# Two inverse transforms on TensorE: one 128-column stationary operand per half of 64 rows, in place of two 64x64 quarters

## The chip, the cores and the metric

The kernel runs on one core of a Trainium2 chip. The metric is the device time of one execution in microseconds (us), the median over several runs. The core has a matrix engine (TensorE, PE in the profile, with its loads of the stationary operand kept apart as PEld), a vector engine (VectorE, DVE), a scalar engine (ScalarE, ACT), GpSimd (POOL) and SyncE (SP), whose queue here issues most DMAs.

## What is computed

A filter in the frequency domain, followed by a gated convolution, for 8 sequences of 3200 positions with 256 channels:

```python
X = np.fft.rfft(x, axis=1)
Yr = Xr @ w_r - Xi @ w_i + b_r
Yi = Xr @ w_i + Xi @ w_r + b_i
Yr = np.sign(Yr) * np.maximum(np.abs(Yr) - 0.01, 0.0)      # and the same for Yi
y = np.fft.irfft(Yr + 1j * Yi, n=3200, axis=1)

for k in range(5):                                          # causal, over positions
    gate_pre += conv_w[k] * yp[:, k:k + S, :]
gate = 1.0 / (1.0 + np.exp(-gate_pre))
out = (gate * (y @ w_val)) @ w_out
```

Inputs and outputs are float32.

## The kernel before

The transform of 3200 points is split into 64 x 50. Per batch (`b`, 8 of them) the work goes through five stages; every stage is a list of *pieces*, and the names in brackets are the tiles that the profile shows.

- `p1` (L529, in the first batch `p1_first`, L486): 50-point transforms of the input, 8 pieces (u) per batch. TensorE writes `p` (L543) with 64x64 quarters: a stationary operand of 50 rows and 64 columns, four of which take up the array, and 512 moving columns. ACT copies `p`, and the result goes to DRAM (`a_dram`).
- `p2` (L564), 13 pieces per batch: `a` comes back from DRAM turned round; 64-point transforms (`s`, L590); the mix with `w_r` and `w_i` (`k_ps` L665, `y_ps` L660), bias and shrinkage on DVE and ACT. These matmuls take the whole array, 128 rows by 128 columns.
- `s1i` (L692, inside `p2`): the first transform back, one group for two pieces, 6 per batch. It writes `z_ps` (L703), in two banks. The stationary operand comes from `g1_sb` (two transforms i, in rows 0 to 63 and 64 to 127), the moving one is `tp` with 256 columns. Each product is split in quarters: half of the rows i, half of the columns e. Two products (r = 0 and 1, real and imaginary) are added up. ACT copies `z_ps` to `z_t` (L714), and a DMA stores it to `z_dram`.
- `positions` (L735), 8 blocks (k) per batch: `zl` comes from `z_dram`; `s2i` (L750) is the second transform back into `y_p` (L759). Here the data are the stationary operand: 50 rows in either half h of the array (`half(h)` is the 50 rows from row 64h), 128 channels of one c and one m split in two quarters e, and the 50x50 matrix `g2_sb` moves. ACT copies `y_p` to `y_sb` (L766).
- `gated` (L827): `v_ps` and `o_ps` (L791; in the last blocks L787) on TensorE, five taps of the convolution on ACT and DVE (L810, L813), the gate (L855), and the store.

Both halves of `z_ps` and of `y_p` write different PSUM banks: `p[:, i, ...]` in `s1i`, `pv[h]` in `s2i`. The tag `ps_2` has two slots of two banks, shared by `p`, `z_ps`, `y_p`, `v_ps` and `o_ps`.

The order on each engine is fixed by the program. `Plan.order` (L111) simulates the pieces with a table of costs and of due times (`O`, L230) and then writes them out; each piece is added with its planned time (1776 ns for `s1i`, 950 ns for `s2i`) and a mode, "q" for the pieces of quarters (`p1`, `s1i`, `s2i`) and "f" for full-size matmuls; the planner charges for a switch from one mode to the other (`SWITCH`, L212) and puts "q" pieces next to each other where it can. The change leaves these planned times and modes alone.

Of the kernel before, what the change touches and what calls it, by code (L numbers as in the profile page):

```python
# [17 lines left out]
B, S, D = 8, 3200, 256  # L18
P = 128
HP = P // 2  # L20
# [59 lines left out]
class Plan:  # L80
# [11 lines left out]
    def add(self, at, engine, busy, fn, uses=(), sets=(), new=None, delay=None, mode="r", kb=0, chain=None, extra=0):  # L92
        n = len(self.pieces)
        before = set()
        for key in uses:
            before |= set(self.writers.get(key, ()))
        for key in sets:
            before |= set(self.readers.get(key, ())) | set(self.writers.get(key, ()))
        for key in uses:
            self.readers.setdefault(key, []).append(n)  # L100
        for key in sets:
            self.writers[key], self.readers[key] = [n], []
        p = dict(n=n, at=at, engine=engine, busy=busy, fn=fn, before=before, new=new or {}, mode=mode, kb=kb, extra=extra,
                 tiles={key[:2] for key in (*uses, *sets)}, delay=busy + LAND[engine] if delay is None else delay)
        p["behind"] = {self.last[chain]} if chain in self.last else set()
        if chain:
            self.last[chain] = n
        self.pieces.append(p)
        return n
# [113 lines left out]
def act(n, kind="copy"):  # L223
    return {"copy": 45, "cast": 95, "mul": 104, "conv": 187, "relu": 198, "sigmoid": 103}[kind] + n / 1.2
# [38 lines left out]
def fourier_filter_then_gated_conv(ctx: ExitStack, tc: tile.TileContext, x, w_r, w_i, b_r, b_i,  # L263
                                   w_val, conv_w, w_out, f1, f2, g1, g2, eye, out):
    nc = tc.nc
# [7 lines left out]
    tl = {}  # L273
# [9 lines left out]
    g2_sb = const.tile([P, N2], F32, name="g2_sb")  # L283
# [10 lines left out]
    def buffer(key, tag, shape, dtype=F32):  # L294
        pool = ps if tag.startswith("ps_") else dram if tag.endswith("_dram") else sb
        tl[key] = pool.tile(shape, dtype, name=key[0], tag=tag, bufs=SLOTS[tag])
        return tl[key]
# [7 lines left out]
    def two_banks(key):  # L305
        return buffer(key, "ps_2", [P, 2, 512])
# [172 lines left out]
    def half(h):  # L479
        return slice(h * HP, h * HP + N2)  # L480
# [83 lines left out]
    def p2(b, u, at):  # L564
# [123 lines left out]
        kts = [("tp", (b, v)) for v in both]  # L688
# [3 lines left out]
        def s1i():  # L692
            p = two_banks(kz)
            if last:
                nc.tensor.matmul(p[:, 0, 0:D], g1_sb[:, ts[0] * P:(ts[0] + 1) * P], tl[kt][:, 0, :], start=True, stop=True)
                return
            for j, v in enumerate(both):
                g = g1_sb[:, 2 * v * P:(2 * v + 2) * P].rearrange("p (r q) -> p r q", r=2)

                for r in range(2):  # L700
                    for i in range(2):
                        for e in range(2):
                            nc.tensor.matmul(p[e * HP:(e + 1) * HP, i, j * D:(j + 1) * D],  # L703
                                             g[i * HP:(i + 1) * HP, r, e * HP:(e + 1) * HP],
                                             tl[kts[j]][i * HP:(i + 1) * HP, r, :], start=r == 0, stop=r == 1)
        add(at + O["s1i"], "PE", 430 if last else 1776, s1i, [*[k + (0,) for k in kts], *gs], [kz + (0,)], {kz: "ps_2"}, mode="f" if last else "q")

        def keep():
# [26 lines left out]
    def positions(b, k, at):  # L735

        bk = (b, k)
        kz, kp = ("zl", bk), ("y_p", bk)

        def load():  # L740
            zt = buffer(kz, "zl", [P, MB * D]).rearrange("p (m c) -> p m c", m=MB)
            src = tl["z_dram", b].rearrange("(f h) (m c) -> h f m c", h=NH, c=D)
            for h in range(NH):
                nc.sync.dma_start(out=zt[half(h)], in_=src[h, :, k * MB:(k + 1) * MB, :])
        add(at + O["load_z"], "SP", 700, load, [("z_dram", b, u) for u in range(NU)], [kz + (0,)], {kz: "zl"}, kb=400, chain="zl")

        def views():
            return [tl[kp][:, h, 0:TB].rearrange("p (c m n) -> p c m n", c=2, m=MB) for h in range(NH)]

        def s2i():  # L750
            zt = tl[kz].rearrange("p (m c) -> p m c", m=MB)
            two_banks(kp)
            pv = views()

            for c in range(2):
                for m in range(MB):
                    for h in range(NH):
                        for e in range(2):
                            nc.tensor.matmul(pv[h][e * HP:(e + 1) * HP, c, m, :],  # L759
                                             zt[half(h), m, c * P + e * HP:c * P + (e + 1) * HP], g2_sb[half(h), :],  # L760
                                             start=True, stop=True)

        free = [("turn", "read", (b - 1, j)) for j in range(4)] if k == NB - 1 and b else []
        add(at, "PE", 950, s2i, [kz + (0,), ("g2", 0, 0), *free], [kp + (0,)], {kp: "ps_2"}, mode="q", chain="s2i")
        lo = (k * MB + H0) * N2
        add(at + 0.1, "ACT", act(2 * TB), lambda: nc.scalar.copy(  # L766
            out=y_sb[:, :, :, lo:lo + MB * N2], in_=tl[kp][:, :, 0:TB].rearrange("p h (c n) -> p c h n", c=2)),
            [kp + (0,)], [("y", k, 0)])
        if k < NB - 1:
            return  # L770
        w = H0 * N2
        add(at + 0.1, "DVE", 283, lambda: nc.vector.tensor_copy(out=y_sb[:, :, 1, 0:w], in_=y_sb[:, :, 0, lo:lo + w]),
            [("y", k, 0)], [("y", -1, 0)])

        def turned(c):
            old = y_sb[:, c, 1, lo:lo + w].rearrange("p (m n) -> p m n", n=N2)
            new = y_sb[:, c, 0, 0:w].rearrange("p (m n) -> p m n", n=N2)
            nc.vector.tensor_copy(out=new[:, :, 1:], in_=old[:, :, :N2 - 1])
        for c in range(2):
            add(at + 0.1, "DVE", 171, lambda c=c: turned(c), [("y", k, 0)], [("y", -1, 1 + c)])  # L780
# [158 lines left out]
    for b in range(B):  # L939
# [11 lines left out]
        start = (b + 1) * T + O["p3"] + O.get(f"p3_{b}", 0.0)  # L951
# [33 lines left out]
```

## Time and profile before

| | |
|---|---|
| median of 3 runs | 900.42 us (905.22, 896.17, 900.42) |
| span of the profiled execution, first to last instruction | 897.1 us |
| mean granted TensorE clock | 0.986 |
| TensorE busy / VectorE / ScalarE | 865.2 / 763.5 / 603.7 us |
| `z_ps` (L703) records on TensorE | 1536 |
| `y_p` (L759) records on TensorE | 4096 |

The profile is one execution of its own. Its time outside the span isn't listed; its span lies 3.3 us below the median of the runs. In it, every fp32 matmul of the program (the two transforms back, `p`, `s`) appears as two matmuls, each with a load of its stationary operand (LDWEIGHTS); a matmul on operands of type fp32r (L660, L665, L791) appears once. Matmuls overlap each other, so their durations don't add up to time; the length of a piece in the chain of waits does. A row like `50*64 50x64` gives rows and columns of the array that are used, then the operand.

### The profile page before, as it was taken

What the parts mean: (1) busy time and instruction counts of PE and PEld (TensorE: products, weight loads), DVE (VectorE), ACT (ScalarE), POOL (GpSimd) and SP (SyncE); (2) the same over time, 40 slices, a digit from 0 to 9 for tenths busy, and PEclk for the clock granted to TensorE, in tenths of its full rate; (3) what the DMA queues carried; (4) which work ended last, traced back from release to release, by engine and by line L of the source; (5) the groups of instructions that cost most, each with busy time, mean ns of one, the idle gap of its engine ahead of it and who ended that gap; (6) DMA issues with size and microseconds to landing.
All of it is one profiled execution on the core that took longest, in us unless ns stands there. A gap on an engine that the chain in (4) does not pass through costs nothing.

```text
span 897.1 us, 24381 instructions
## 1 busy us (share of the span) xinstructions
PE 865.2 (96%) x10370; PEld 741.1 (83%) x10370; DVE 763.5 (85%) x1139; ACT 603.7 (67%) x924; POOL 4.4 (0%) x11
## 2 busy tenths in 40 slices
PE   7799979999999999999999999999999999999898
PEld 2478758898888988899888988989788899998675
DVE  1267787999899997999789996999969998999896
ACT  1256656877677867777677876877757776875654
POOL 0000000000000000000000000000001000000000
PEclk8889999999999999999999999999999999999999
DMA  6577777635755476555674566645674453513522
GB/s 203 198 233 239 228 227 217 210 130 182 236 180 179 159 229 218 190 183 160 217 235 158 163 204 217 222 131 174 215 223 154 139 172 109 178 62 116 180 75 91
DMA packets 103439, 162.26 MB, mean 181 GB/s; under 512 B 9154, under 2 KB 77636, under 8 KB 103332
## 3 DMA queue, kind: packets, MB, share of 16 engines
q1 hardware_dynamic: 102372, 157.44, 54.8%
q10 hardware_dynamic: 960, 3.28, 1.1%
q8 instruction: 81, 1.33, 0.6%
q14 instruction: 26, 0.21, 0.1%
HBM read 82.04 MB, written 78.64 MB: 179 GB/s over the span
## 4 chain that ended last, share of the span: by engine, by line
PE 83%; DVE 10%; DMA 4%; ACT 2%; issue 1%; ACTq 1%; SPq 0%
PE y_ps L660 14%; PE o_ps L791 13%; PE v_ps L791 12%; PE s L590 10%; PE z_ps L703 9%; PE k_ps L665 8%; PE y_p L759 7%; PE p L543 6%; DVE acc L813 4%; DMA x<-in_x 1%; PE v_ps L787 1%; DVE acc L855 1%; DVE gated L317 1%; DMA f_sb<-in_f 1%; DMA a_dram<-s 1%
## 5 line engine op out<-in xcount | busy, mean ns | idle before, releaser
L813 DVE SCALAR_TENSOR_TENSOR acc<-y_sb,cw_sb,acc 128x800 f32<-128x800 f32 (+1 forms) x264 | 255.9, 1018 | 17.6 <-ACT acc L810 17.2
L660 PE MATMUL y_ps<-w_sb,xs 128*128 128x256 f32 x1152 | 155.4, 284 | 0.6 <-DVE xs L648 0.6
L791 PE MATMUL o_ps<-gated,wo_sb 128*128 128x400 f32 x756 | 155.2, 351 | 0.6 <-DVE acc L855 0.6
L660 PEld LDWEIGHTS y_ps<-w_sb,xs 128*128 128x128 f32 x1152 | 144.5, 189 | 11.3 <-DVE xs L652 3.2
L791 PEld LDWEIGHTS o_ps<-gated,wo_sb 128*128 128x128 f32 x756 | 133.5, 188 | 3.1 <-DVE acc L855 0.8
L791 PE MATMUL v_ps<-y_hl,wv_sb 128*128 128x400 f32 x660 | 131.3, 346 | 0.5 <-ACT o L879 0.5
L590 PE MATMUL s<-f_sb,a 128*128 128x128 f32 x800 | 113.2, 284 | 8.2 <-ACT wo_sb L315 3.4
L791 PEld LDWEIGHTS v_ps<-y_hl,wv_sb 128*128 128x128 f32 x660 | 118.5, 188 | 1.6 <-ACT o L879 0.9
L590 PEld LDWEIGHTS s<-f_sb,a 128*128 128x128 f32 x800 | 101.7, 196 | 20.8 <-issue 6.9
L678 ACT ACTIVATE tp<-yb,nlam 128x512 f32<-128x512 f32 (+1 forms) x104 | 73.7, 708 | 38.7 <-DVE yb L674 38.6
L665 PEld LDWEIGHTS k_ps<-w_sb,xs 128*128 128x128 f32 x576 | 77.2, 190 | 20.8 <-issue 10.5
L703 PE MATMUL z_ps<-tp,g_sb 64*64 64x256 f32 x1536 | 93.4, 381 | 0.0
L665 PE MATMUL k_ps<-w_sb,xs 128*128 128x256 f32 x576 | 91.1, 294 | 1.2 <-DVE yb L671 0.9
L759 PEld LDWEIGHTS y_p<-g_sb,zl 50*64 50x64 f32 x4096 | 68.3, 135 | 18.1 <-issue 7.3
L315 ACT CAST gated<-acc 128x800 fp32r<-128x800 f32 x63 | 54.3, 862 | 38.2 <-DVE acc L855 38.0
L759 PE MATMUL y_p<-g_sb,zl 50*64 50x50 f32 x4096 | 72.5, 219 | 7.1 <-issue 4.2
L680 DVE SCALAR_TENSOR_TENSOR tp<-yb,tp 128x512 f32<-128x512 f32 (+1 forms) x104 | 70.0, 673 | 10.6 <-ACT tp L678 10.5
L671 DVE TENSOR_TENSOR yb<-k_ps,bias_sb 128x512 f32<-128x512 f32 x96 | 65.6, 684 | 15.7 <-PE k_ps L665 15.6
L703 PEld LDWEIGHTS z_ps<-tp,g_sb 64*64 64x64 f32 x1536 | 55.3, 133 | 27.4 <-issue 5.1
L855 DVE TENSOR_TENSOR acc<-v_ps,acc 128x800 f32<-128x800 f32 x64 | 62.9, 984 | 16.1 <-PE v_ps L791 12.7
L674 DVE TENSOR_TENSOR yb<-y_ps,yb 128x512 f32<-128x512 f32 x96 | 65.5, 683 | 7.4 <-PE y_ps L660 6.9
L714 ACT COPY z_t<-z_ps 128x1024 f32<-128x1024 f32 x48 | 48.5, 1010 | 25.7 <-PE z_ps L703 25.1
(80 smaller groups left out, 1016.7 us busy)
## 6 DMA issues: line engine op xcount, KB each, us to landing
zl<-z_dram SPq DMA_DIRECT2D x128, 200.0 KB
out<-o SPq DMA_DIRECT2D x63, 400.0 KB
a<-a_dram SPq DMA_DIRECT2D x96, 256.0 KB
z_dram<-z_t SPq DMA_DIRECT2D x48, 512.0 KB
x<-in_x SPq DMA_DIRECT2D x120, 200.0 KB
a_dram<-s SPq DMA_DIRECT2D x120, 200.0 KB
x<-in_x ACTq DMA_DIRECT2D x8, 200.0 KB
a_dram<-s ACTq DMA_DIRECT2D x8, 200.0 KB
```

Source lines behind the costliest of these rows:

```text
L590: nc.tensor.matmul(spec()[:, c, :, i, :], tl[ka][:, i, c * P:(c + 1) * P], f2_of(i), start=True, stop=True)
L660: nc.tensor.matmul(p[:, 1 - r, :], xm(hx, c, r), w_sb[:, m, hw, c, :], start=k == 0, stop=k == 5)
L665: nc.tensor.matmul(p, sm(hx, c), w_sb[:, 0, hw, c, :], start=k == 0, stop=k == 5)
L671: nc.vector.tensor_tensor(out=buffer(kb, "yb", [P, 2, D]), in0=tl[kk].rearrange("p (a d) -> p a d", a=1).to_broadcast([P, 2, D]), in1=bias ...
L674: add(at + 0.2, "DVE", dve(2 * D), lambda: nc.vector.tensor_tensor(out=yb(), in0=tl[ky], in1=yb(), op=ALU.add), [ky + (0,)], [kb + (0,)])
L678: nc.scalar.activation(out=buffer(kt, "tp", [P, 2, D])[:, 0:n], in_=tl[kb][:, 0:n], func=AF.Relu, bias=nlam)
L680: add(at + 0.2, "DVE", dve(n * D), lambda: nc.vector.scalar_tensor_tensor(out=tl[kt][:, 0:n], in0=tl[kb][:, 0:n], scalar=LAM, in1=tl[kt][: ...
L703: nc.tensor.matmul(p[e * HP:(e + 1) * HP, i, j * D:(j + 1) * D], g[i * HP:(i + 1) * HP, r, e * HP:(e + 1) * HP], tl[kts[j]][i * HP:(i + 1) ...
L759: nc.tensor.matmul(pv[h][e * HP:(e + 1) * HP, c, m, :], zt[half(h), m, c * P + e * HP:c * P + (e + 1) * HP], g2_sb[half(h), :], start=True ...
L791: nc.tensor.matmul(p[:, e, 0:TB], w[:, hw, c, e * P:(e + 1) * P], src(hy, c), start=n == 0, stop=n == 5)
L813: nc.vector.scalar_tensor_tensor(out=acc(c), in0=y_of(c, j), scalar=cw_sb[:, c, j:j + 1], in1=acc(c), op0=ALU.mult, op1=ALU.add)
L855: add(at + O["gate"], "DVE", dve(2 * TB), lambda: nc.vector.tensor_tensor(out=gate(), in0=hn(tl[kv][:, :, 0:TB]), in1=gate(), op=ALU.mult) ...
```

## The change

Where `s1i` and `s2i` issued two matmuls for the two halves e of the stationary operand's columns, they issue one with all 128 columns, in the same half of rows. The output of each goes to all 128 partitions of PSUM. The sums, their order and the data are the same.

```diff
@@ s1i
                 for r in range(2):
                     for i in range(2):
-                        for e in range(2):
-                            nc.tensor.matmul(p[e * HP:(e + 1) * HP, i, j * D:(j + 1) * D],
-                                             g[i * HP:(i + 1) * HP, r, e * HP:(e + 1) * HP],
-                                             tl[kts[j]][i * HP:(i + 1) * HP, r, :], start=r == 0, stop=r == 1)
+                        nc.tensor.matmul(p[:, i, j * D:(j + 1) * D], g[i * HP:(i + 1) * HP, r, :],
+                                         tl[kts[j]][i * HP:(i + 1) * HP, r, :], start=r == 0, stop=r == 1)
@@ s2i
             for c in range(2):
                 for m in range(MB):
                     for h in range(NH):
-                        for e in range(2):
-                            nc.tensor.matmul(pv[h][e * HP:(e + 1) * HP, c, m, :],
-                                             zt[half(h), m, c * P + e * HP:c * P + (e + 1) * HP], g2_sb[half(h), :],
-                                             start=True, stop=True)
+                        nc.tensor.matmul(pv[h][:, c, m, :], zt[half(h), m, c * P:(c + 1) * P], g2_sb[half(h), :], start=True, stop=True)
```

Nothing moves against anything else on any engine; the groups at the two lines have half as many matmuls with twice the columns. The rows of TensorE's program, in the first batch where `z_ps` stands between two groups of `p` (a row gives line, tile and operands, output shape and the number of the program's matmuls in a row). Before:

```order
L424 MATMUL turned<-eye_sb,f_sb 128x128 x2
L543 MATMUL p_796<-x,f_sb 64x512 x4
L703 MATMUL z_ps<-tp,g_sb 64x256 x16
L543 MATMUL p_832<-x,f_sb 64x512 x4
L665 MATMUL k_ps<-w_sb,xs 128x256 x6
```

and with the change:

```order
L424 MATMUL turned<-eye_sb,f_sb 128x128 x2
L543 MATMUL p_772<-x,f_sb 64x512 x4
L702 MATMUL z_ps<-tp,g_sb 128x256 x8
L543 MATMUL p_800<-x,f_sb 64x512 x4
L665 MATMUL k_ps<-w_sb,xs 128x256 x6
```

The places are the same; `z_ps` has outputs of 128 partitions now, while its neighbours `p` keep 64. Later, in a batch with `y_p` groups, next to each other and next to `p`. Before:

```order
L660 MATMUL y_ps<-w_sb,xs 128x256 x12
L759 MATMUL y_p<-g_sb,zl 64x50 x64
L665 MATMUL k_ps<-w_sb,xs 128x256 x6
L759 MATMUL y_p<-g_sb,zl 64x50 x32
L543 MATMUL p_5702<-x,f_sb 64x512 x4
L590 MATMUL s_5712<-f_sb,a 128x2x64 x4
```

and with the change:

```order
L660 MATMUL y_ps<-w_sb,xs 128x256 x12
L756 MATMUL y_p<-g_sb,zl 128x50 x32
L665 MATMUL k_ps<-w_sb,xs 128x256 x6
L756 MATMUL y_p<-g_sb,zl 128x50 x16
L543 MATMUL p_5062<-x,f_sb 64x512 x4
L590 MATMUL s_5072<-f_sb,a 128x2x64 x4
```

A group of `y_p` has 16 matmuls in place of 32, at the same place. Over the whole program there are 64 groups of `y_p` and 48 of `z_ps` of this form, 33 of the latter right behind full-size matmuls; a group of `p` comes right behind one of them 24 times, and one of them right behind `p` 12 times.

## Prediction, made before the changed kernel ran

> **What bounds the kernel now.** I read the page's first part, the busy time by stretch, and then the chain of waits for the stretch in which the two transforms back run. First the page:
>
> ```profile
> span 897.1 us, 24381 instructions
> PE 865.2 (96%) x10370; PEld 741.1 (83%) x10370; DVE 763.5 (85%) x1139; ACT 603.7 (67%) x924; POOL 4.4 (0%) x11
> ```
>
> TensorE leads, but VectorE at 85% could be the limit somewhere. The view by stretch separates the two; its columns are the stretch, its length, then each engine's busy time with the number of its instructions, the granted clock and the DMA share:
>
> ```profile
> 60.00:100.00 40.00, 40.00 (x408) 33.63 (x407) 25.12 (x46) 26.83 (x48) 0.00 (x0) 1.00 0.75 237
> ...
> 300.00:400.00 100.00, 100.00 (x1281) 88.98 (x1280) 91.12 (x134) 74.59 (x114) 0.00 (x0) 1.00 0.61 194
> ...
> 700.00:800.00 100.00, 99.51 (x1433) 93.53 (x1431) 94.23 (x139) 71.34 (x113) 0.00 (x0) 1.00 0.44 141
> 800.00:870.00 70.00, 64.90 (x834) 53.72 (x834) 66.34 (x82) 44.61 (x59) 0.00 (x0) 1.00 0.36 118
> ```
>
> A busy TensorE may still be one that is not needed, so the chain of waits decides. Its summary for 135 to 794 us, and for 794 to 868 us:
>
> ```profile
> by line: PE y_ps L660 17.0%; PE v_ps L791 16.6%; PE o_ps L791 16.1%; PE s L590 11.8%; PE z_ps L703 10.9%; PE k_ps L665 9.6%; PE y_p L759 8.2%; PE p L543 6.0%; issue 0.7%; PE y_ps L623 0.7%; PE y_ps L624 0.6%; PE z_ps L695 0.4%; DVE gated L3
> ...
> by line: DVE acc L813 44.0%; DVE acc L855 11.4%; DVE gated L317 8.2%; PE y_p L759 6.0%; issue 4.9%; ACT acc L824 4.3%; DVE y_hl L317 4.1%; DVE tp L680 3.2%; ACT acc L810 2.6%; DVE yb L674 2.5%; DVE yb L671 1.6%; DVE xs L648 1.6%; ACT y_sb L
> ```
>
> In the long middle the chain is TensorE line after line: whatever a group there takes more or less moves the end by as much. In the 74 us of the second row VectorE leads and TensorE waits, apart from the y_p groups (6.0%). Both edited lines, L703 and L759, stand on the first chain.
>
> **The edit itself** replaces two matmuls of 64 stationary columns by one of 128. For each of the two, the question is what a step costs: the moving operand streaming through, or the stationary operand being loaded. From the view of groups by line:
>
> ```profile
> L590 PE MATMUL s<-f_sb,a 128*128 128x128 f32 x800 | 113.2, 284 | 8.2 <-ACT wo_sb L315 3.4
> L590 PEld LDWEIGHTS s<-f_sb,a 128*128 128x128 f32 x800 | 101.7, 196 | 20.8 <-issue 6.9
> L703 PE MATMUL z_ps<-tp,g_sb 64*64 64x256 f32 x1536 | 93.4, 381 | 0.0
> L703 PEld LDWEIGHTS z_ps<-tp,g_sb 64*64 64x64 f32 x1536 | 55.3, 133 | 27.4 <-issue 5.1
> L759 PE MATMUL y_p<-g_sb,zl 50*64 50x50 f32 x4096 | 72.5, 219 | 7.1 <-issue 4.2
> L759 PEld LDWEIGHTS y_p<-g_sb,zl 50*64 50x64 f32 x4096 | 68.3, 135 | 18.1 <-issue 7.3
> ```
>
> The profile counts two matmuls and two loads for each fp32 matmul of the program: 48 groups of 32 at L703, 64 groups of 64 at L759. The means are durations with a fixed delay in them, not costs in a stream. Costs in a stream come from the chain, where consecutive pieces add up without overlap (start, length, what):
>
> ```profile
> 72.31 1.73 PE z_ps L703 x32
> ...
> 401.51 0.89 PE s L590 x8
> ...
> 403.80 1.89 PE z_ps L703 x32
> 405.69 0.92 PE y_p L759 x64
> 406.61 1.09 PE s L590 x8
> ...
> 423.53 1.02 PE p L543 x8
> 424.55 1.61 PE y_ps L660 x12
> ...
> 428.05 0.86 PE p L543 x8
> 428.91 0.90 PE k_ps L665 x6
> ...
> 432.89 1.40 PE y_ps L660 x12
> ...
> 436.48 0.70 PE k_ps L665 x6
> ```
>
> **The z_ps step is streaming.** With four quarters side by side a group has 8 steps: 1.73 / 8 = 0.216 us. The s row streams 128 columns in 0.89 / 8 = 0.111 us at most, so 256 columns need about 0.22. Nothing is left over for loading. With two halves side by side there are again 8 steps of 256 columns. The load of 128 columns, at most the 0.111 of an s step, fits behind 0.216. I take zero for the stream; the bounds are zero and the 0.111 of an uncovered load per step, and that end is a rival below.
>
> **The y_p step is loading.** 64 records are 16 steps of four quarters: 0.92 / 16 = 0.0575 us. Streaming 50 columns at the s rate is 50/128 of 0.111 = 0.043, so it doesn't fill the step. The timeline of the loads alone, in windows that widen, shows what does (start, from the first start to the last end, number):
>
> ```profile
> 403.73 0.15 PEld L703 LDWEIGHTS z_ps<-tp,g_sb 64*64 64x64 f32 x4
> ...
> 403.73 0.21 PEld L703 LDWEIGHTS z_ps<-tp,g_sb 64*64 64x64 f32 x8
> ...
> 406.54 0.19 PEld L590 LDWEIGHTS s<-f_sb,a 128*128 128x128 f32 x1
> ...
> 406.54 0.30 PEld L590 LDWEIGHTS s<-f_sb,a 128*128 128x128 f32 x2
> ```
>
> Four loads of 0.133 end within 0.15, so they start within 0.02 of each other, and the next four end 0.06 later. A load of 128 columns ends 0.11 behind the one before. The durations agree: 196 - 133 = 63 ns more for 64 more columns. So 64 columns cost about 0.055, and four such loads are done in 0.06: they run at the same time, the two quarters of one half of rows included. One load of 128 columns in place of that pair does one after the other what was done at once: about 0.111 in place of 0.0575. The program's group keeps 16 steps (two halves in place of four quarters), so it becomes 16 x 0.111 = 1.78 us, **0.86 more**. Bounds for a step: 0.043, the streaming, below which nothing goes, and 0.222, two loads of halves in series. I take 0.111, because the nearest row, the s load, has the same type and the same 128 columns.
>
> The Trainium skill's page "TensorE: Matmul & The Clock Gate", section "LDWEIGHTS (loading the stationary operand)", gives columns / 1.2 ns whatever the number of rows; an estimate from it is 107 ns for 128 columns and 53 for 64, and the load rows above agree. By it the step would gain 0.05 and the sum be 4 us lower. The page "TensorEngine Tiling (Array Packing)", section "Restrictions", speaks for the change: tiling by columns switches Fast Weight Load off. The first page allows that mode only for types other than FP32, and the s loads, 128 columns without column tiles, show no trace of it; if it held here, the time would be that of the first rival below.
>
> How many groups count? The view of L759 alone by stretch:
>
> ```profile
> 100.00:800.00 700.00, 62.98 (x3584) 59.84 (x3584) 1.00 0.58 185
> 800.00:868.00 68.00, 9.54 (x512) 8.46 (x512) 1.00 0.37 122
> ```
>
> 3584 / 64 = 56 groups lie before 800, on TensorE's chain. Of the 8 behind, these are on the chain:
>
> ```profile
> 834.09 2.08 PE y_p L759 x128
> 836.19 1.19 PE y_p L759 x64
> ...
> 855.39 1.19 PE y_p L759 x64
> ```
>
> Those are four; the other four stand beside VectorE's taps (L813) and are covered. 60 x 0.86 = **51.6 us**. If none of the last eight counted it would be 48.2, with all of them 55.0.
>
> **Switches of shape.** In the chain rows a group of quarters behind full-size matmuls costs 0.16 more (p 1.02 against 0.86, z_ps 1.89 against 1.73), and full-size matmuls behind quarters 0.20 more (k_ps 0.90 against 0.70, s 1.09 against 0.89, y_ps 1.61 against 1.40). Today p, z_ps and y_p have one shape; afterwards p keeps its quarters and the others have halves. By the order of the program on TensorE there are 36 places where p meets one of them, 24 into p and 12 out of it. The trace has no switch between quarters and halves. It is bounded by nothing and by these rows; I take the rows, since the switch today changes both sizes and its cost depends on the width loaded next: 24 x 0.16 + 12 x 0.20 = **6.2 us**. The 33 z_ps groups behind full-size matmuls load 128 columns first, 0.04 more each by the same two rows: **1.3 us**.
>
> **What hides nothing.** ACT's copy of y_p (L766) starts 0.86 later, and behind it in ACT's queue stand the casts and the first tap. In the middle ACT is busy 75 of 100 us and TensorE has other groups in line, so I cost it at nothing; without that cover TensorE would wait out another 0.86 per group, up to 52 us. Half the instructions at the edited lines save no time, since neither step is limited by issue.
>
> **The sum.** 51.6 + 6.2 + 1.3 = 59.1 us on the profiled span of 897.1, so 956.2. The listed runs are 905.22, 896.17 and 900.42 us; the profiled execution lies 3.3 below their median, and I carry that offset: **960 us**.
>
> **Rivals.**
> *The load is no longer the limit (faster).* Should a half's 128 columns load in 0.043 or less, y_p steps become streaming: 16 x (0.043 - 0.0575) = -0.23 a group, -14 over 60, and 887 us if the switches cost nothing. It decides at the 0.0575 that a step takes today. For it speaks only that no load in this shape is in the trace; against it the 0.11 of the s load, which holds in a stream. 0.04.
> *The change doesn't change the step.* If the two quarters of a half already loaded in turn, at 0.028 each, the load of 128 columns takes the same 0.0575. Only 36 switches at 0.16 stay: 906 us. Against it: 0.028 for 64 columns would be half the s load's rate. 0.06.
> *Halves in series.* If loads of the two halves can't run at once, a y_p step is 0.222: 16 x (0.222 - 0.0575) x 60 = +158; z_ps loads just fit. With the switches 1066 us. The trace has no halves; that quarters of different rows load at once speaks against it. 0.04.
> *A load can't begin while its own half streams.* Then y_p steps are 0.111 + 0.043 = 0.154, +93 us, and z_ps steps get 0.111 more, 8 x 0.111 x 48 = +43; 1043 us with the switches. The z_ps steps speak against it: 0.216 is all streaming, with 256 columns and a load in it. 0.04. The page on TensorE, section "What overlaps and what doesn't", states just this rule, that a load overlaps matmuls only of another row group; this trace disagrees with it, by that 0.216.
>
> **How the numbers follow.** The forecast has 0.82. Its own range: without switches and with none of the last eight groups 900.4 + 48.2 + 1.3 = 950; the 0.30 - 0.19 = 0.11 of the loads' timeline, good to its last digit, leaves a step of 0.107 open, 4 us less in all, 946; and the listed runs scatter by 5 either way: 940 at the low end. With all eight groups 963, with scatter 968, and with a fifth of ACT's 52 us uncovered 980. That leaves the rivals' 0.18 out, so it is the whole range. A difference under about 1% can't be told from none here. Faster by over 1%: 0.04; within 1%: 0.06; slower by over 1%: 0.90.
>
> **What will show it.** Behind the change y_p should have 2048 records, loads of about 190 ns, and groups of 32 in about 1.8 us of the chain; z_ps groups 16 records in 1.7 to 1.9 as now; p groups behind z_ps 1.02 in place of 0.86. VectorE's share should fall to about 80%. The forecast is wrong if y_p groups stay near 0.9, or z_ps groups leave 1.9.

## The result, and the profile after

The changed kernel takes 962.25 us (median of 4 runs, 959.2 to 966.26), the kernel before 898.84 us in the same comparison: a ratio of 1.0689, interval 1.0621 to 1.0757. The profiled execution has a span of 958.7 us in a run of 960.48. The page's first part, and its groups at the two edited lines (`y_p` is L756 now, `z_ps` L702):

```profile
span 958.7 us, 18749 instructions
PE 935.2 (98%) x7554; PEld 817.4 (85%) x7554; DVE 767.2 (80%) x1139; ACT 609.5 (64%) x924; POOL 4.4 (0%) x11
...
L756 PEld LDWEIGHTS y_p<-g_sb,zl 50*128 50x128 f32 x2048 | 123.8, 193 | 11.2 <-DVE yb L674 3.2
...
L702 PE MATMUL z_ps<-tp,g_sb 64*128 64x256 f32 x768 | 95.6, 388 | 0.0
...
L702 PEld LDWEIGHTS z_ps<-tp,g_sb 64*128 64x128 f32 x768 | 70.2, 186 | 18.1 <-issue 5.1
```

There are half as many records at both lines, and each load takes 186 to 193 ns where it took 133 to 135. VectorE, with nearly the same work (767.2 us for 763.5), is busy for 80% of the longer span. What that costs in a stream is in the chain of waits (start, length, what):

```profile
402.14 1.93 PE z_ps L702 x16
404.06 1.02 PE p L543 x8
405.08 0.91 PE k_ps L665 x6
...
415.25 1.60 PE y_ps L660 x12
416.85 1.92 PE y_p L756 x32
418.77 1.79 PE z_ps L702 x16
420.56 1.72 PE y_p L756 x32
```

Two `y_p` groups in a row, and one behind full-size matmuls, first in the kernel before, then in the changed one:

```profile
248.64 2.01 PE y_p L759 x128
...
251.55 1.08 PE y_p L759 x64
```

```profile
258.04 3.71 PE y_p L756 x64
...
262.64 1.92 PE y_p L756 x32
```

A `y_p` group takes 1.72 us behind `z_ps`, where it took 0.92, and 1.92 behind full-size matmuls, where it took 1.08. In a row of two, the second takes 3.71 - 1.92 = 1.79, where it took 2.01 - 1.08 = 0.93. A `z_ps` group takes 1.79 behind halves, nearly the 1.73 it took behind quarters: its stream didn't change. `p` behind `z_ps` takes 1.02 where it took 0.86.

Two things are not in the prediction's sum. The first is the clock that TensorE is granted. A table by stretch (start and end, length, TensorE busy, its loads, DVE, ACT, POOL, granted clock, DMA):

```profile
366.00:369.40 3.40, 3.40 (x61) 3.34 (x60) 2.58 (x6) 1.71 (x4) 0.00 (x0) 1.00 0.61 196
369.40:379.60 10.20, 10.20 (x61) 8.27 (x62) 5.00 (x6) 5.43 (x8) 0.00 (x0) 0.50 0.49 148
888.10:894.90 6.80, 6.80 (x43) 6.67 (x42) 1.91 (x2) 3.36 (x4) 0.00 (x0) 0.51 0.52 162
898.30:905.20 6.90, 6.90 (x29) 6.11 (x28) 6.69 (x7) 3.88 (x5) 0.00 (x0) 0.51 0.56 176
```

TensorE is busy all through the first row and its clock falls to half behind it. The chain has the same stretches, each right behind two or three `y_p` groups in a row:

```profile
365.64 3.71 PE y_p L756 x64
369.35 1.49 PE k_ps L665 x6
370.84 3.59 PE y_p L756 x32
...
884.29 6.94 PE y_p L756 x96
891.23 4.14 PE o_ps L786 x12
```

`k_ps` takes 1.49 for its 0.7 to 0.9, `o_ps` 4.14 for its 2.17. These three stretches, some 24 us at half speed, are 12 us lost; a fourth, short one follows the two groups at 912.16 (a clock of 0.63 between 916 and 920).

Two things limit this reading. The kernel before loses to the clock too: in its first 140 us, and once in the middle (0.62 between 663.0 and 666.5, behind a stop of 1.32). By the mean clocks of the two profiled executions, 0.977 of 958.7 us and 0.986 of 897.1, the loss grows from 12.6 to 22.0 us, by some 9.5. And not every run of two groups is followed by half clock: those at 258.04, 589.49, 699.05, 804.64 and 846.12, 3.71 us each, are not. What decides between them wasn't followed up.

The second is a stop that is gone. TensorE's largest wait in the kernel before, from its view of waits (total, times, longest), was for "issue", which means that it waited for nothing that the profile shows. Behind it, one of these stops in the chain:

```profile
PE y_p L759 <- issue: 4.2, 4, 1.5
...
453.55 1.07 PE y_p L759 x60
454.62 1.49 issue
456.10 0.32 PE y_p L759 x3
```

Four times, for 1.5 us at most, it stood still in the third `y_p` group of a batch, which comes behind two in a row and six `k_ps`. In other batches the same group went through (the 1.08 at 251.55 above). The changed kernel has no such row at `y_p`; these groups have half the instructions.

### The profile page after: what moved, and what is told of

Read it like the earlier page. It is cut to its first block, busy times and chain, and to the rows that moved or that the text cites. A ratio compares the mean times of both kernels' runs of the same rounds, so it can differ in the third digit from the quotient of the medians.

```text
span 958.7 us, 18749 instructions
## 1 busy us (share of the span) xinstructions
PE 935.2 (98%) x7554; PEld 817.4 (85%) x7554; DVE 767.2 (80%) x1139; ACT 609.5 (64%) x924; POOL 4.4 (0%) x11
## 4 chain that ended last, share of the span: by engine, by line
PE 88%; DVE 6%; DMA 3%; ACT 2%; issue 0%; ACTq 0%; SPq 0%
PE y_ps L660 14%; PE o_ps L786 13%; PE y_p L756 13%; PE v_ps L786 12%; PE s L590 10%; PE z_ps L702 9%; PE k_ps L665 8%; PE p L543 6%; DVE acc L808 2%; DMA a_dram<-s 1%; PE v_ps L782 1%; DMA x<-in_x 1%; DVE acc L850 1%; DVE st L356 1%; DMA b_sb<-in_b_i 1%; PE y_ps L623 1%
## 5 line engine op out<-in xcount | busy, mean ns | idle before, releaser
L786 PE MATMUL o_ps<-gated,wo_sb 128*128 128x400 f32 x756 | 160.1, 359 | 0.0
L786 PEld LDWEIGHTS o_ps<-gated,wo_sb 128*128 128x128 f32 x756 | 138.1, 194 | 2.5 <-issue 0.3
L756 PEld LDWEIGHTS y_p<-g_sb,zl 50*128 50x128 f32 x2048 | 123.8, 193 | 11.2 <-DVE yb L674 3.2
L756 PE MATMUL y_p<-g_sb,zl 50*128 50x50 f32 x2048 | 127.2, 277 | 1.5 <-DVE acc L850 1.5
L702 PE MATMUL z_ps<-tp,g_sb 64*128 64x256 f32 x768 | 95.6, 388 | 0.0
L761 ACT COPY y_sb<-y_p 128x800 f32<-128x800 f32 x64 | 53.0, 828 | 54.5 <-PE y_p L756 54.2
L702 PEld LDWEIGHTS z_ps<-tp,g_sb 64*128 64x128 f32 x768 | 70.2, 186 | 18.1 <-issue 5.1
```

The lines of the kernel that those rows point to most:

```text
L702: nc.tensor.matmul(p[:, i, j * D:(j + 1) * D], g[i * HP:(i + 1) * HP, r, :], tl[kts[j]][i * HP:(i + 1) * HP, r, :], start=r == 0, stop=r == 1)
L756: nc.tensor.matmul(pv[h][:, c, m, :], zt[half(h), m, c * P:(c + 1) * P], g2_sb[half(h), :], start=True, stop=True)
L786: nc.tensor.matmul(p[:, e, 0:TB], w[:, hw, c, e * P:(e + 1) * P], src(hy, c), start=n == 0, stop=n == 5)
```

## Experiments

**Each edit alone.** `z_halves` is the kernel before with this edit only:

```diff
-                        for e in range(2):
-                            nc.tensor.matmul(p[e * HP:(e + 1) * HP, i, j * D:(j + 1) * D],
-                                             g[i * HP:(i + 1) * HP, r, e * HP:(e + 1) * HP], ...)
+                        nc.tensor.matmul(p[:, i, j * D:(j + 1) * D], g[i * HP:(i + 1) * HP, r, :], ...)
```

> Only the first transform back (z_ps) takes 128 columns; y_p keeps its quarters. Theory (a step of z_ps is streaming; a switch between quarters and halves costs what one between quarters and full size costs): z_ps groups take 1.93 us in the chain whatever stands ahead of them, p and y_p groups behind z_ps 0.16 more than now. 8 switches into z_ps from p and 7 from y_p at 0.20, 18 into p and 19 into y_p at 0.16, 33 longer first loads at 0.04: 4.3 + 4.6 + 1.3 = 10 us, a ratio of 1.011. TensorE's stops for 'issue' in y_p, some 4 us in all, stay. Rival (the switch between quarters and halves is free): ratio 1.00, and p behind z_ps stays at 0.86.

Measured: 909.06 us against 900.14, ratio 1.0099 (1.0066 to 1.0131). From its chain:

```profile
402.51 1.08 PE y_p L757 x64
...
435.56 1.93 PE z_ps L702 x16
437.49 1.02 PE p L543 x8
```

`y_p` behind `z_ps` costs 1.08 where it cost 0.92, `p` 1.02 where it cost 0.86, and `z_ps` 1.93. A switch between quarters and halves costs as much as one between quarters and full size. By count these switches come to 10 us, and the medians differ by 8.9: they are enough to explain what the first edit costs. The sum isn't exact, since the profiled execution also waits 6.8 us for one DMA near its start, where the kernel before waited 2.0, and its stops at `y_p` are 2.0 us, where 4 were expected to stay.

`y_halves` has the other edit only, in `s2i`:

```diff
-                        for e in range(2):
-                            nc.tensor.matmul(pv[h][e * HP:(e + 1) * HP, c, m, :],
-                                             zt[half(h), m, c * P + e * HP:c * P + (e + 1) * HP], g2_sb[half(h), :], ...)
+                        nc.tensor.matmul(pv[h][:, c, m, :], zt[half(h), m, c * P:(c + 1) * P], g2_sb[half(h), :], ...)
```

> Only the second transform back (y_p) takes 128 columns; z_ps keeps its quarters. Theory (the load of the stationary operand sets the y_p step, 0.107 in place of 0.0575 us): y_p groups 1.7 to 1.95 us, 49 us over 60 groups; 36 switches round y_p 6 us; the stops for 'issue' go (-4); half-clock stretches appear as with the whole change (+10). About 960 us, a ratio of 1.065 to 1.07, nearly the whole loss. Rival (the loss is spread over both edits): 930 to 940.

Measured: 965.76 us, ratio 1.0717 (1.0649 to 1.0785). The loss sits in `y_p`. From its chain:

```profile
415.56 1.92 PE y_p L758 x32
417.49 1.89 PE z_ps L703 x32
419.37 1.92 PE y_p L758 x32
```

The two ratios exceed 1 by 8.2% together, the whole change by 6.9%. Where `z_ps` and `y_p` meet, each edit alone makes a switch that both together don't (1.92 for `y_p` behind `z_ps` here, 1.72 above): 26 places at 0.16 to 0.20 in either kernel, 9 us in the two, or 1% of the time. The rest of the 1.3% isn't split: the ratios are good to 0.3 and 0.7%, and the profiled `y_halves` lost more to the clock (0.970) than the whole change (0.977).

**What sets the step, and what drops the clock.** `wide_halves` changes the moving operand in the changed kernel:

```diff
-                        nc.tensor.matmul(pv[h][:, c, m, :], zt[half(h), m, c * P:(c + 1) * P], g2_sb[half(h), :], start=True, stop=True)
+                        lo = (c * MB + m) * N2
+                        w = g2_sb[half(h), :].rearrange("p (a n) -> p a n", a=1).to_broadcast([N2, 2, N2])
+                        nc.tensor.matmul(tl[kp][:, h, lo:lo + 2 * N2].rearrange("p (a n) -> p a n", a=2), zt[half(h), m, c * P:(c + 1) * P], w, start=True, stop=True)
```

> The whole change, and y_p's moving operand is g2 twice over, 100 columns; the second 50 results of each matmul are overwritten by the next one, so the output stays. Theory (loading sets the y_p step at 0.107, streaming of 50 columns fills 0.042 of it): 100 columns stream in 0.083 and still fit, y_p groups stay at 1.72 to 1.95. Theory on the clock (TensorE's granted clock falls to half because y_p streams for only 40% of the time): with 78% it doesn't fall any more, and the 24 us more of half clock go, about 12 us: 950 us, a ratio of 1.055. Rival to the first (streaming sets the step): groups take 0.8 more, over 1000 us. Rival to the second (the clock falls for another reason): 962 us with the same stretches at half clock.

Measured: 952.69 us, ratio 1.0578 (1.0530 to 1.0626). From its chain:

```profile
414.70 1.96 PE y_p L758 x32
416.66 1.75 PE z_ps L702 x16
418.42 1.76 PE y_p L758 x32
```

Twice the streaming costs 0.04 a group, about what 50 more columns take once (an estimate from the 0.086 us for 100 columns below), so streaming isn't the limit in the halves. What is left is the load. And with twice the streaming the kernel is *faster* than the changed one. The clock row of the page's second part (forty slices of the span, tenths of full speed), the changed kernel first, then this one:

```profile
PEclk9799999999999997999999999999999999999799
```

```profile
PEclk9789999999999999999999999999999999999999
```

The two 7s in the middle and at the end are gone; the low digits at the start, while the first loads are awaited, stay. The medians lie 9.6 us apart, although every group is 0.04 longer (2.4 us in 60). They come from two comparisons whose intervals just touch, so the size is less sure than the cause. The cause rests on every run: the mean clock was 0.983 to 0.990 in six runs of this kernel, against 0.967 to 0.977 in four of the changed one and 0.962 to 0.978 in six of `y_halves`. Against the changed kernel, the steps and the number of matmuls are the same and the streaming is doubled: TensorE's clock fell because `y_p` streamed too little, not because TensorE waited.

`wide_quarters` does the same to the kernel before.

> The kernel before with y_p's moving operand at 100 columns, the second 50 results overwritten by the next matmul. Theory (a y_p step of quarters is a load of 0.0575, just over the streaming of 0.042): 100 columns need 0.083 to 0.087 and become the limit, 16 x 0.028 = 0.45 us a group, 27 us over 60 groups, 925 us, a ratio of 1.03. Rival (something else sets the step, with room to spare): no change.

Measured: 921.75 us, ratio 1.0242 (1.0190 to 1.0294). From its chain:

```profile
401.65 1.38 PE y_p L761 x64
```

1.38 / 16 = 0.086 us a step, streaming of 100 columns; the same addition that is free in halves costs 0.46 a group in quarters. That would be 28 us for 60 groups; 21.6 were measured, with an interval of 17 to 26. The stops at `y_p` are 2.1 us here, for 4.2; the rest of the difference wasn't followed up.

**Do the loads of the quarters run at the same time?** Two orders of the kernel before's own `y_p` matmuls. `one_quarter`:

```diff
-            for c in range(2):
-                for m in range(MB):
-                    for h in range(NH):
-                        for e in range(2):
+            for h in range(NH):
+                for e in range(2):
+                    for c in range(2):
+                        for m in range(MB):
```

> The kernel before with y_p's 32 quarter matmuls ordered so that all 8 of one quarter follow each other before the next quarter begins; same matmuls, same results. Theory (64 columns take 0.055 us to load, and the four quarters load at once): one quarter alone takes a step of about 0.0575 for each matmul record, so a group of 64 records takes 64 x 0.0575 = 3.7 us in place of 0.92. Rival (64 columns load in 0.028 and the two quarters of a half take turns): the step falls to the streaming of 50 columns, 0.043, and a group takes 2.8 us.

Measured in one execution: 1101.51 us. From its chain, and from its timeline in windows that widen, well inside a quarter (start, from the first start to the last end, number):

```profile
422.97 3.13 PE y_p L759 x64
```

```profile
423.81 0.39 PE L759 MATMUL y_p<-g_sb,zl 50*64 50x50 f32 x4
...
423.81 0.57 PE L759 MATMUL y_p<-g_sb,zl 50*64 50x50 f32 x7
```

Three records more take 0.18, or 0.06 each: one quarter alone has the step of four quarters together, so the load of 64 columns costs it the same. The group misses 3.7 by 0.6, which neither theory foresaw: where one quarter ends and the next begins, the start times run as two interleaved series of 0.058, three records long. By these times the next quarter begins before the last one is through, which saves about 0.2 at each of the three borders.

`one_half` puts only h outermost:

```diff
-            for c in range(2):
-                for m in range(MB):
-                    for h in range(NH):
+            for h in range(NH):
+                for c in range(2):
+                    for m in range(MB):
                         for e in range(2):
```

> The kernel before with y_p's quarter matmuls ordered so that all of one half of rows come before the other half; the two quarters of the half alternate. Theory (both quarters of a half load at the same time): a pair of records per 0.0575, 32 pairs, 1.84 us a group. Rival (the quarters of a half load in turn, 0.055 each): 3.7 us, as with one quarter alone.

Measured in one execution: 946.57 us. From its chain:

```profile
425.33 1.66 PE y_p L759 x64
```

32 pairs in 1.66 us: less than half of the 3.7 that loads in turn would take, and under the 1.84 of the theory by 0.18, the same saving at the one border between the halves. Two quarters of one half of rows load at the same time. That is the gain that the change gave up.

**More of the same.** If column tiles load at once, eight tiles should load faster than four. `eight_tiles`:

```diff
-                        for e in range(2):
-                            nc.tensor.matmul(pv[h][e * HP:(e + 1) * HP, c, m, :],
-                                             zt[half(h), m, c * P + e * HP:c * P + (e + 1) * HP], g2_sb[half(h), :],
+                        for e in range(4):
+                            nc.tensor.matmul(pv[h][e * 32:(e + 1) * 32, c, m, :],
+                                             zt[half(h), m, c * P + e * 32:c * P + (e + 1) * 32], g2_sb[half(h), :],
```

> The kernel before with y_p in eight tiles of 64 rows by 32 columns, so that eight loads of 32 columns can run at once; twice the instructions. Theory (load time goes with the columns of one load, and different column tiles load at once): a load takes 0.028, the step falls to the streaming of 50 columns, 0.042 to 0.045, a group to 0.7 us: 12 us faster, 888 us, ratio 0.987. Rival (16 instructions in a step can't be issued in 0.045; the matmuls of a step of quarters start 0.0065 apart, eight of them would need 0.052 and the eight loads beside them more): 0.92 a group or slower, and more stops for 'issue' since there are 128 records where 64 were: ratio 1.00 to 1.06.

Measured: 984.73 us, ratio 1.0946 (1.0858 to 1.1034): my theory's forecast was wrong, and the ratio lies above the rival's range (1.00 to 1.06) too. Its waits and a piece of its chain:

```profile
PE y_p L759 <- issue: 33.1, 24, 4.2
```

```profile
424.04 0.21 PE y_p L759 x7
424.25 0.50 issue
424.75 1.33 PE y_p L759 x77
```

The rival's signs are there: slower groups and more stops. Beside the stop this group of 128 records takes 0.21 + 1.33 = 1.54 us on the chain (which passes over some of its records), where quarters take 0.92. The loads did get shorter (112 ns a record, for 135). Right behind the stop, at a granted clock of 1.00, the timeline has 7 matmuls ending by 425.02 and 21 by 425.09: 0.04 for eight, as my theory had it. Later in the same group it has 40 by 425.52 and 60 by 425.71: 0.076 for eight. TensorE's "issue" waits at `y_p` are 33 us, where they were 4. I read this as instructions that run short, since the theory's step holds only right behind a stop; and `one_quarter` and `one_half`, which spread the quarters' number of instructions over longer groups, have no "issue" row at `y_p`. How much of the loss is the issue within a group, the stops, or the lower clock (0.949 over the run) wasn't tried apart. No experiment points to a kernel faster than the one before.

## Why the prediction was right

960 us was forecast with 940 to 980, and 962.25 measured. By its own steps:

- *The `y_p` step is loading.* Right, and shown: 0.112 (1.79 / 16, the second group of a row of two) against a forecast of 0.111. Behind `z_ps` a group shows less, 1.72, since its first matmuls start under the end of `z_ps`: the timeline has them at 420.40, 0.16 before the chain counts them. Extra streaming is free in halves and not in quarters; one quarter alone keeps the step of four. A group grew by 0.80 behind `z_ps`, 0.84 behind full-size matmuls and 0.85 in a row of two (3.71 against 2.01), for a forecast of 0.86: some 50 us over the 60 groups for 51.6. The estimate by the page "TensorE: Matmul & The Clock Gate" of the Trainium skill, section "LDWEIGHTS (loading the stationary operand)", 107 ns for 128 columns and 53 for 64, lies 5 ns below the measured steps of 112 and 58 (0.93 / 16).
- *The `z_ps` step is streaming.* Right: 1.79 behind halves for 1.73 behind quarters, and the edit alone costs its switches (1.0099).
- *Switches.* Right in size: 1.02 for `p` behind `z_ps`, 1.93 for `z_ps` behind full size, where 1.89 stood.
- *"Half the instructions at the edited lines save no time."* Wrong by the 4.2 us of stops that went. The row was in the trace of before, at a line that the prediction quotes; I read the step's limit and not the supply of instructions over a run of three groups.
- *The clock.* Missing in the sum. I took it as it was, while the change halves the share of time in which `y_p` streams: some 9.5 us between the two profiled executions, net of what the kernel before loses to its own clock. `wide_halves` gives 9.6 between medians.
- *ACT's copy.* I costed its later start at nothing, and the waits bear that out: the changed kernel's only row of a wait at `y_p` is 1.5 us for DVE, where the kernel before had 2.2 for DVE and 0.7 for ACT.
- *The last eight groups.* I put four on the chain: too few. All are on it now. The chain's shares on the page, before and after, and its `y_p` rows behind 890 us:

```profile
PE 83%; DVE 10%; DMA 4%; ACT 2%; issue 1%; ACTq 1%; SPq 0%
```

```profile
PE 88%; DVE 6%; DMA 3%; ACT 2%; issue 0%; ACTq 0%; SPq 0%
...
895.37 4.15 PE y_p L756 x64
...
912.16 4.21 PE y_p L756 x64
...
927.49 1.95 PE y_p L756 x32
```

With the 6.94 at 884.29, three groups, these are the eight, part of them at half clock. VectorE's taps, which ended last there before, now end earlier than TensorE, and VectorE lost 4 points of the chain.

So the total of 61.6 us between the two spans (59.1 forecast) is a mechanism sized nearly right and two missed terms of opposite sign: 50 for `y_p`, 7.5 for the switches, 9.5 for the clock and -4.2 for the stops come to some 63. How many of the last eight groups count isn't known to better than some 3 us. That the mechanism came out is no luck; that the median came out within 3 us is, since the missed terms partly cancel. The rivals fell: `y_p` did slow down, the halves do load at once (16 steps of 0.112, not 32), and a load doesn't wait for its own half's stream, which would have made 0.15 of it. One reading in the prediction is slightly off: for the rival with the halves in series, two loads of 0.111 don't quite fit behind a `z_ps` step of 0.216, which would add some 2 us to its 1066.

## What to carry to other kernels

With short moving operands, look at what a step waits for before merging matmuls. Where it was the load of the stationary operand here, two narrow column tiles that load at once beat one wide load (0.058 a step for 0.112); where it was streaming, the merge changed only the switches of shape at its edges. Count these switches by the order on the engine, and price them from two rows of the same group behind different neighbours. Fewer instructions paid off a little here (4 us of stops), and twice as many cost more than the shorter loads could have saved, so look for TensorE's "issue" waits in both directions.

## What was not expected of the hardware

TensorE's granted clock fell to half while TensorE had no gap: behind 3.7 us and more of `y_p` halves (0.112 a step, some 0.043 of it streaming, by the 0.086 for 100 columns), though not behind every such run, and behind none of them with twice the streaming in the same step. With one quarter of the array at a time the mean granted clock of the one execution was 0.912, against 0.986. And by their start times, matmuls of one tile can start before earlier ones of another tile: with one quarter after the other, three of 16 records overlapped. The records don't name the tile; it is inferred from the two series.
